# Splitting the spectrum tile z: the upper fifteen frequencies in a tile of their own, by channel

## Chip, core and metric

The kernel runs on one core of a Trainium2 chip. The metric is device time in microseconds of one execution. The engines are named as the profile names them: PE multiplies matrices (PEld is its load of the stationary operand), DVE, ACT and POOL work on elements, SP issues most of the transfers. ACT and POOL issue some too, and that time is not counted as busy.

## The reference

Four batches of 10048 positions and 128 channels go through a gated long convolution and then a hierarchical mixture of experts:

```
u = x * v
y = irfft(rfft(u, 2S) * rfft(h_filt, 2S))[:S]      # per channel, h_filt from a small network
x = x * y                                          # 40192 rows of 128
group = argmax(x @ w_group); expert = argmax(x @ w_expert[group])
out = g_w * e_w * (relu(x @ w1[expert]) @ w2[expert])
```

## The kernel before

A sequence is cut into 79 blocks of 128 positions, and the transform is done in two factors by matrix products in fp32. `dft_blocks` takes three channels a step (43 steps for 128 channels): 12 matmul instructions against `self.fa` turn 96 blocks into 79 complex numbers each, 158 columns per channel, in a tile `psa` of PSUM. One copy (L397) then writes them to `self.z`, a tile of [128 positions, 80 frequencies, 2 parts, 128 channels]; the 80th frequency is zero. `middle` takes two frequencies a step: `dft_positions` (L471) multiplies the 256 numbers of each frequency in z, as moving operand, by `bt`, then DVE and POOL multiply by the spectrum of the filter, and `back` (L641) multiplies by `bp` and copies the result back to z (L648, ACT).

The way back needs z with frequencies on the partitions. `turned` does this for 12 channels at a time. For the frequencies below KM = 64 it is one transpose of 128x128 for each channel (L671): 64 frequencies with two parts are 128 rows. The upper 16 frequencies of a channel are 32 rows, and four channels are put on top of each other by four matmuls against the identity, each into 32 partitions (L661). PE records two instructions for each of those fp32 matmuls and one for a transpose. The turned blocks lie in `pt` (three buffers, shared by others of the pool `psT`) and go by ACT (L673) to `tt`: first the upper frequencies of all 12 channels, 384 columns, then three blocks of 512. `inverse_blocks` (L696, L704) multiplies `tt` by `self.fi` into `po`, ACT makes `oo` of it (L713, L714), DVE `yt` and the product `xy` (L719, L721).

The stages follow each other. The network of the filter, its transform and its spectrum come first, then the transform of batch 0 and its middle. For each further batch one mixed stage does the transform of that batch (L392, L442, L453, L455 prepare it) together with the way back of the batch before, and a middle follows, with the routing of the batch before in it. After the last middle only the way back of batch 3 is left, and then the experts, page by page of 256 rows. For the text below: F is the filter's transform (43 to 78 us), D the transform of batch 0 (118 to 176), M0 to M3 the middles (176, 361, 586 and 822 on), X1 to X3 the mixed stages (250 to 361, 466 to 586, 695 to 822), T the last way back (924 to 999), E the experts (1029 on).

The order on an engine is made when the program is built, except where a line fixes it: the framework lets an instruction overtake others of its engine where data allow. Waits between engines follow from the tiles.

Of the kernel before, what the change touches and what calls it, by code (L numbers as in the profile page):

```python
# [12 lines left out]
F32 = mybir.dt.float32  # L13
# [12 lines left out]
SEQ, D, NB, N1 = 10048, 128, 79, 157  # L26
KM = 64
# [105 lines left out]
def groups(n, step):  # L133
    return [(i, min(step, n - i)) for i in range(0, n, step)]
# [5 lines left out]
class Kernel:  # L140
# [60 lines left out]
    def conv(self, ctx, right):  # L201
        tc, nc, d = self.tc, self.nc, self.d
        cp = ctx.enter_context(tc.tile_pool(name="cconst", bufs=1))
        zp = ctx.enter_context(tc.tile_pool(name="z", bufs=1))
# [3 lines left out]
        self.psr = lambda shape, name: self.psO.tile(shape, F32, tag="po", name=name)  # L208
        self.fa = cp.tile([NR, 2, 2 * NB], F32, name="fa")

        self.z = zp.tile([128, KM + 16, 2, 128], F32, name="z")
        nc.vector.memset(self.z[:, NB:], 0.0)
        ahead = ExitStack()
        made, folded = [], []
        with ExitStack() as c2:
# [12 lines left out]
        for b in range(self.nbat + 1):  # L228
# [41 lines left out]
            if not last:  # L270
                back = []
                for i, (k0, n) in enumerate(groups(NB, 2)):
                    back.append(self.middle(b, k0, n))
                    if len(back) > LAG:
                        self.back(*back.pop(0))
                    if b == 1 and i % 4 == 1:
                        self.clear_rest(i // 4)
                    self.scatter(i % 4 != 3)
                    if i % 4 != 3 if i < 30 else i % 2:
                        next(routing, None)  # L280
                for args in back:
                    self.back(*args)
# [101 lines left out]
    def dft_blocks(self, b, eo, d0, n, other=False):  # L384

        nc = self.nc
        pool, tag = (self.psA, "ps") if b not in ("h", 0) or d0 // GD % 2 else (self.psT, "pt")
        ps = pool.tile([128, GD, 2 * NB], F32, tag=tag, name="psa")
        for i in range(n):

            for h, hs in enumerate(HALVES):
                nc.tensor.matmul(  # L392
                    ps[hs, i], eo[:, i, hs], self.fa[:, h], start=True, stop=True
                )
        copy = nc.vector.tensor_copy if other else nc.scalar.copy

        ins = copy(  # L397
            self.z[:, :NB, :, d0 : d0 + n].rearrange("p k s d -> p (k s) d"),
            ps[:, :n].rearrange("p d c -> p c d"),
        )  # L400
        self.pace = ins
        self.in_turn(b, ins)
        self.tc.declare_no_dep(ins.ins, group=f"z{b}", reason="every step has channels of its own")
        self.tc.add_to_no_dep_group(f"z{b}", ins.ins)

    def run_ahead(self, b, i, made, folded):

# [57 lines left out]
    def dft_positions(self, k0, n, bt, other=False):  # L465

        nc = self.nc
        pool, tag = (self.psT, "pt") if other else (self.psA, "ps")
        ps = pool.tile([128, 2, 2, 128], F32, tag=tag, name="psb")
        for i in range(n):  # L470
            nc.tensor.matmul(  # L471
                ps[:, i],
                bt[:, i],
                self.z[:, k0 + i],
                start=True,
                stop=True,
            )
        return ps

    def parts(self, pool, src, tag, bufs=1, lo=None):  # L480

        nc, shape = self.nc, list(src.shape)
        parts = [pool.tile(shape, F32R, tag=f"{tag}{i}", name=f"{tag}{i}", bufs=bufs) for i in range(2)]
        nc.scalar.copy(parts[0], src)
        (lo or nc.gpsimd).tensor_tensor(parts[1], src, parts[0].bitcast(F32), ALU.subtract)
        return parts
# [149 lines left out]
    def back(self, k0, n, bp, y):  # L636

        nc = self.nc
        po = self.psT.tile([128, 2, 2, 128], F32, tag="pt", name="pbp")
        for i in range(n):  # L640
            nc.tensor.matmul(  # L641
                po[:, i].rearrange("p s d -> p (s d)"),
                bp[:, i],
                y[:, i].rearrange("p s d -> p (s d)"),
                start=True,
                stop=True,
            )
        self.pace = nc.scalar.copy(self.z[:, k0 : k0 + n], po[:, :n])  # L648

    def turned(self, d0, n):  # L650


        nc = self.nc
        tts = []
        for s, m in [(None, n // 4)] + groups(n, 4):
            pt = self.psT.tile([128, 4, 128], F32, tag="pt", name="pt")
            for i in range(m):
                if s is None:

                    for c in range(4):  # L660
                        nc.tensor.matmul(  # L661
                            pt[32 * c : 32 * c + 32, i],
                            self.z[:, KM:, :, d0 + 4 * i + c].rearrange("p k s -> p (k s)"),
                            self.ident,
                            start=True,
                            stop=True,
                            tile_position=(0, 32 * c),
                        )
                else:
                    src = self.z[:, :KM, :, d0 + s + i].rearrange("p k s -> p (k s)")  # L670
                    nc.tensor.transpose(pt[:, i], src, self.ident)  # L671
            tt = self.sp.tile([128, 4, 128], F32, tag="tt", name="tt", bufs=NTT)
            nc.scalar.copy(tt[:, :m], pt[:, :m])  # L673
            tts.append(tt)
        return tts
# [748 lines left out]
```

## Time and profile before

| | us |
|---|---|
| median of 3 runs | 2085.32 (2081.45 to 2090.16) |
| profiled execution | 2083.48 |
| its span | 2081.7 |

| engine | busy us | share |
|---|---|---|
| PE | 1962.0 | 94% |
| PEld | 1803.8 | 87% |
| DVE | 1626.1 | 78% |
| ACT | 1444.8 | 69% |
| POOL | 1333.4 | 64% |

Half of the span is stage E, where PE hardly pauses. The other half is the convolution, with four kinds of stages whose limits differ, so that the shares above say little: a stage is read by its own windows, and within it by who waits for whom. The busy time of PE in a window is the union of its instructions; the end of a matmul is modelled and contains the time until its last column is out.

### The profile page before, as it was taken

The numbers are of one execution on the slowest core, as the hardware profiler recorded it, in microseconds if no ns is written. First come the engines' busy times: TensorE is split into PE (matmuls) and PEld (weight loads), VectorE is DVE, ScalarE is ACT, GpSimd is POOL, SyncE is SP. The second block draws the span as 40 slices with busy tenths as digits, with TensorE's granted clock in tenths as the row PEclk, the third lists the DMA queues.
The fourth block names the chain that finished last, engine by engine and source line by source line (L and its number), as shares of the span: only waits on it lengthen the run. The fifth ranks groups of instructions, "written<-read, shape, count | busy, mean of one in ns | idle before, by whom it ended". The sixth has DMA issues, their size and how long they took to land.

```text
span 2081.7 us, 54011 instructions
## 1 busy us (share of the span) xinstructions
PE 1962.0 (94%) x18062; PEld 1803.8 (87%) x18062; DVE 1626.1 (78%) x3432; ACT 1444.8 (69%) x3210; POOL 1333.4 (64%) x1371
## 2 busy tenths in 40 slices
PE   8988999979999789989899999999999999999997
PEld 7867888767787578768699999999999999999997
DVE  5587765687658765796599998889999998888885
ACT  6652477436753466436688788888888888888886
POOL 3157600665689657976357677888888886555554
PEclk9999999999999799999899999999999999999999
DMA  4699965976889578968544455555555554443442
GB/s 136 226 263 267 275 168 160 333 226 174 229 301 296 157 190 254 339 198 277 188 126 136 134 154 151 155 180 169 157 161 155 161 150 131 125 134 121 127 126 66
DMA packets 258721, 388.93 MB, mean 187 GB/s; under 512 B 32680, under 2 KB 132627, under 8 KB 258433
## 3 DMA queue, kind: packets, MB, share of 16 engines
q1 hardware_dynamic: 225024, 318.01, 50.8%
q0 software_dynamic: 23904, 51.83, 7.0%
q10 hardware_dynamic: 9504, 15.54, 2.8%
q8 instruction: 146, 2.39, 0.5%
q14 instruction: 143, 1.16, 0.2%
HBM read 303.24 MB, written 83.04 MB: 186 GB/s over the span
## 4 chain that ended last, share of the span: by engine, by line
PE 50%; DVE 2%; POOL 2%; issue 1%; DMA 1%; ACT 0%; SPq 0%; DVEq 0%; ACTq 0%; POOLq 0%
PE py L1293 7%; PE py L1291 7%; PE py L1292 7%; PE ph L1272 7%; PE ph L1274 7%; PE ph L1273 7%; PE ptm L1305 2%; PE px L1229 2%; POOL wl L1261 1%; POOL out L1317 1%; PE pt L671 1%; PE ptr L786 1%; PE po L696 0%; PE po L704 0%; DMA mw<-m_w 0%
## 5 line engine op out<-in xcount | busy, mean ns | idle before, releaser
L1281 DVE SCALAR_TENSOR_TENSOR hl<-ph,hh 128x512 fp32r<-128x512 f32 x656 | 445.2, 683 | 93.3 <-ACT hh L1280 92.5
L1280 ACT ACTIVATE hh<-ph 128x512 fp32r<-128x512 f32 x656 | 395.6, 603 | 138.8 <-PE ph L1274 71.9
L358 POOL DMA_INDIRECT prow<-stg,adr x316 | 355.1, 1124 | 136.4 <-issue 63.6
L1317 POOL DMA_INDIRECT out<-os,to x328 | 349.0, 1064 | 91.6 <-issue 72.5
L1291 PE MATMUL py<-hh,wh 128*128 128x256 f32 x1312 | 398.7, 304 | 0.0
L1272 PE MATMUL ph<-xh,wh 128*128 128x256 f32 x1312 | 373.5, 285 | 5.4 <-ACT wh L1254 2.8
L1293 PE MATMUL py<-hh,wl 128*128 128x256 f32 x1312 | 373.2, 284 | 5.5 <-POOL wl L1261 5.5
L1274 PE MATMUL ph<-xh,wl 128*128 128x256 f32 x1312 | 373.4, 285 | 0.4 <-DVE wl L1261 0.4
L1273 PE MATMUL ph<-xl,wh 128*128 128x256 f32 x1312 | 372.9, 284 | 0.0
L1292 PE MATMUL py<-hl,wh 128*128 128x256 f32 x1312 | 371.4, 283 | 0.0
L1261 POOL TENSOR_TENSOR wl<-ws,wh 128x512 fp32r<-128x512 f32 x162 | 220.1, 1359 | 202.1 <-ACT wh L1254 200.9
L1293 PEld LDWEIGHTS py<-hh,wl 128*128 128x128 f32 x1312 | 251.4, 192 | 8.4 <-POOL wl L1261 8.4
L1272 PEld LDWEIGHTS ph<-xh,wh 128*128 128x128 f32 x1312 | 252.8, 193 | 6.1 <-ACT wh L1254 3.0
L1274 PEld LDWEIGHTS ph<-xh,wl 128*128 128x128 f32 x1312 | 253.1, 193 | 0.9 <-DVE wl L1261 0.8
L1273 PEld LDWEIGHTS ph<-xl,wh 128*128 128x128 f32 x1312 | 253.2, 193 | 0.1
L1292 PEld LDWEIGHTS py<-hl,wh 128*128 128x128 f32 x1312 | 252.8, 193 | 0.0
L1291 PEld LDWEIGHTS py<-hh,wh 128*128 128x128 f32 x1312 | 252.0, 192 | 0.0
L1261 DVE TENSOR_TENSOR wl<-mw,wh 128x512 fp32r<-128x512 f32 x328 | 238.1, 726 | 0.0
L648 ACT COPY z<-pbp 128x512 f32<-128x512 f32 (+1 forms) x160 | 92.6, 579 | 207.1 <-PE pbp L641 204.2
L630 POOL TENSOR_TENSOR y<-t 128x256 f32<-128x256 f32 (+1 forms) x160 | 121.2, 757 | 159.5 <-DVE t L629 153.9
L471 PE MATMUL psb<-z,bt 128*128 128x256 f32 x790 | 201.1, 387 | 8.6 <-DMA bt<-c_b 2.8
L1254 ACT CAST wh<-mw 128x512 fp32r x328 | 206.6, 630 | 0.0
(232 smaller groups left out, 4339.7 us busy)
## 6 DMA issues: line engine op xcount, KB each, us to landing
ws<-m_w SPq DMA_DIRECT2D x328, 256.0 KB
ht<-hspec SPq DMA_DIRECT2D x156, 256.0 KB
xv<-xv_in SPq DMA_DIRECT2D x131, 288.0 KB
bt<-c_b SPq DMA_DIRECT2D x95, 256.0 KB
xg<-prow SPq DMA_DIRECT2D x164, 130.0 KB
bp<-c_bp SPq DMA_DIRECT2D x76, 256.0 KB
stg<-xyd SPq DMA_DIRECT2D x76, 256.0 KB
xyd<-xy SPq DMA_DIRECT2D x57, 256.0 KB
```

The source lines that it names most:

```text
L358: ins = self.nc.gpsimd.indirect_dma_start(self.d["prow"], bass.IndirectOffsetOnAxis(ap=u.adr[:, t : t + 1], axis=0), u.rows[:, t - u.t0], ...
L1254: k.fix(k.nc.scalar.copy(hi, self.matrix(i, half, self.ea)))
L1261: ins = v.tensor_tensor(lo, self.matrix(i, half, self.ed), self.wh[i][half].bitcast(F32), ALU.subtract)
L1272: k.fix(nc.tensor.matmul(ph[:, j], wh, self.xh, start=True, stop=False))
L1273: k.fix(nc.tensor.matmul(ph[:, j], wh, self.xl, start=False, stop=False))
L1274: k.fix(nc.tensor.matmul(ph[:, j], wl, self.xh, start=False, stop=True))
L1280: k.fix(nc.scalar.activation(hh, ph, AF.Relu))
L1281: k.fix(nc.vector.scalar_tensor_tensor(hl, ph, 0.0, hh.bitcast(F32), ALU.max, ALU.subtract))
L1291: k.fix(nc.tensor.matmul(self.py, wh, self.hh[c], start=(c == 0), stop=False))
L1292: k.fix(nc.tensor.matmul(self.py, wh, self.hl[c], start=False, stop=False))
L1293: k.fix(nc.tensor.matmul(self.py, wl, self.hh[c], start=False, stop=(c == NC - 1)))
L1317: ins = k.nc.gpsimd.indirect_dma_start(k.d["out"], bass.IndirectOffsetOnAxis(ap=self.to[:, h : h + 1], axis=0), o[:, h], None, bounds_chec ...
```

## The change

The tile z keeps the 64 lower frequencies, in the layout that it had. The upper 15, and a sixteenth that is zero, move to a new tile `zr` of [128 positions, 128 channels, 16 frequencies, 2 parts]. For four channels its 128 numbers then lie next to each other, and one transpose turns them. Both tiles together have the size of z before.

- `dft_blocks` copies `psa` in two instructions on the same engine: 384 elements per partition to z, and three runs of 30 to zr.
- `dft_positions` reads a frequency above 63 from zr: 128 pairs, 128 bytes apart. Its result stands in `psb` as before, so that the output of the matmul now goes by channel: neighbouring columns lie 512 bytes apart.
- `back` lays `pbp` out by channel for these frequencies: the matmul's output has a step of 16 bytes, and ACT's copy writes runs of four numbers to zr.
- `turned` issues one transpose for four channels in place of four matmuls.

```
-        self.z = zp.tile([128, KM + 16, 2, 128], F32, name="z")
-        nc.vector.memset(self.z[:, NB:], 0.0)
+        self.z = zp.tile([128, KM, 2, D], F32, name="z")
+        self.zr = zp.tile([128, D, 16, 2], F32, name="zr")
+        nc.vector.memset(self.zr[:, :, NB - KM :], 0.0)
...
-        ins = copy(
-            self.z[:, :NB, :, d0 : d0 + n].rearrange("p k s d -> p (k s) d"),
-            ps[:, :n].rearrange("p d c -> p c d"),
-        )
+        main = self.z[:, :, :, d0 : d0 + n].rearrange("p k s d -> p (k s) d")
+        rest = self.zr[:, d0 : d0 + n].rearrange("p d k s -> p d (k s)")[:, :, : 2 * (NB - KM)]
+        for name, to, at in (
+            ("z", main, ps[:, :n, : 2 * KM].rearrange("p d c -> p c d")),
+            ("zr", rest, ps[:, :n, 2 * KM :]),
+        ):
+            ins = copy(to, at)
...
         for i in range(n):
             nc.tensor.matmul(
-                ps[:, i],
+                self.by_channel(k0, ps)[:, i],
                 bt[:, i],
-                self.z[:, k0 + i],
+                self.frequency(k0 + i),
...
+    def frequency(self, k):
+        return self.z[:, k] if k < KM else self.zr[:, :, k - KM]
+    def by_channel(self, k, t):
+        return t if k < KM else t.rearrange("p i s d -> p i d s")
...
+        po = self.psT.tile([128, 512], F32, tag="pt", name="pbp")
+        if k0 < KM:
+            po = po.rearrange("p (i s d) -> p i s d", i=2, s=2)
+        else:
+            po = po.rearrange("p (d i s) -> p i s d", i=2, s=2)
...
+            to = self.zr[:, :, k0 - KM : k0 - KM + n]
+            self.pace = nc.scalar.copy(to, po[:, :n].rearrange("p i s d -> p d i s"))
...
-                    for c in range(4):
-                        nc.tensor.matmul(
-                            pt[32 * c : 32 * c + 32, i],
-                            self.z[:, KM:, :, d0 + 4 * i + c].rearrange("p k s -> p (k s)"),
-                            self.ident,
-                            start=True,
-                            stop=True,
-                            tile_position=(0, 32 * c),
-                        )
+                    src = self.zr[:, d0 + 4 * i : d0 + 4 * i + 4].rearrange("p d k s -> p (d k s)")
+                    nc.tensor.transpose(pt[:, i], src, self.ident)
```

PE in a mixed stage, at one turn of 12 channels. `psa` is the transform of the next batch, `pt` the turned block, `po` the way back. Before:

```order
L392 MATMUL psa<-fa,eo 64x158 x6
L661 MATMUL pt<-ident,z 32x128 x12
L671 MATMUL pt<-ident,z 128x128 x12
L392 MATMUL psa<-fa,eo 64x158 x6
L696 MATMUL po<-fi,tt 64x316 x2
```

and with the change, at the same place:

```order
L393 MATMUL psa<-fa,eo 64x158 x6
L680 MATMUL pt<-ident,zr 128x128 x3
L683 MATMUL pt<-ident,z 128x128 x12
L393 MATMUL psa<-fa,eo 64x158 x6
L708 MATMUL po<-fi,tt 64x316 x2
```

Twelve matmuls became three transposes, and their neighbours stayed.

ACT in the same stage, from the second `oo` of a turn to the copies of the turned blocks (`tt`). `z` and `zr` are the copies of the transform, `xv` the sign change of the next input. Before:

```order
L714 COPY oo<-po 64x474
L397 COPY z<-psa 128x158x3
L453 ACTIVATE xv<-xv 96x3x64
L673 COPY tt<-pt 128x384
L453 ACTIVATE xv<-xv 96x3x64
L673 COPY tt<-pt 128x512 x3
```

and with the change, in X1 and X2:

```order
L726 COPY oo<-po 64x474
L404 COPY z<-psa 128x128x3
L404 COPY zr<-psa 128x3x30
L685 COPY tt<-pt 128x384
L685 COPY tt<-pt 128x512 x3
L457 ACTIVATE xv<-xv 96x3x64
```

The copy of the transform is two, and both sign changes that stood ahead of the last `tt` copies stand behind them or elsewhere in the turn.

PE at the end of a middle, where the last frequencies pass (`psb` forward, `pbp` back). Before:

```order
L471 MATMUL psb<-z,bt 128x256 x2
L641 MATMUL pbp<-y,bp 128x256 x2
L471 MATMUL psb<-z,bt 128x256 x2
L641 MATMUL pbp<-y,bp 128x256 x2
L471 MATMUL psb<-z,bt 128x256
```

and with the change:

```order
L475 MATMUL psb<-zr,bt 128x128x2 x2
L657 MATMUL pbp<-y,bp 128x2x128 x2
L475 MATMUL psb<-zr,bt 128x128x2 x2
L657 MATMUL pbp<-y,bp 128x2x128 x2
L475 MATMUL psb<-zr,bt 128x128x2
```

The order is the same; the operands are read, and the results written, with steps.

## Rows read from the trace of the kernel before

**Rows 1.** Busy time by stage: window, us, engines in us, granted clock, DMA share.

```profile
core 0: us, PE busy (x) PEld busy (x) DVE busy (x) ACT busy (x) POOL busy (x), PEclk, DMA share, GB/s
...
43.30:78.20 34.90, 34.57 (x512) 34.28 (x512) 14.35 (x22) 13.93 (x22) 0.00 (x0) 1.00 0.34 115
...
117.70:175.60 57.90, 47.98 (x513) 38.00 (x513) 46.62 (x78) 22.70 (x40) 41.57 (x61) 0.94 1.09 252
175.60:250.30 74.70, 70.19 (x318) 59.11 (x318) 54.23 (x87) 23.16 (x42) 57.25 (x82) 1.00 0.87 281
250.30:360.80 110.50, 104.85 (x1577) 92.75 (x1576) 68.40 (x122) 84.75 (x169) 1.42 (x3) 1.00 0.59 165
...
466.20:585.70 119.50, 109.60 (x1577) 96.31 (x1576) 76.52 (x157) 83.45 (x167) 73.61 (x73) 0.96 0.72 201
585.70:695.00 109.30, 94.29 (x585) 72.83 (x581) 87.99 (x187) 41.47 (x98) 96.99 (x117) 0.95 0.88 291
695.00:822.30 127.30, 115.30 (x1580) 99.79 (x1580) 83.44 (x181) 84.76 (x167) 78.80 (x75) 0.91 0.68 191
...
924.20:998.80 74.60, 71.46 (x1068) 60.59 (x1068) 47.43 (x103) 49.10 (x85) 44.24 (x43) 0.97 0.78 256
...
1029.00:2081.70 1052.70, 1028.12 (x8534) 1023.11 (x8534) 909.39 (x1908) 873.68 (x1971) 739.46 (x663) 0.99 0.47 142
```

**Rows 2.** Groups of the convolution, PE: busy us, mean ns, idle before.

```profile
L671 PE MATMUL pt<-ident,z 128*128 128x128 f32 x512 | 97.9, 334 | 26.7 <-ACT tt L673 26.4
...
L671 PEld LDWEIGHTS pt<-ident,z 128*128 128x128 f32 x512 | 82.8, 251 | 38.7 <-ACT tt L673 32.0 <-issue 2.1
...
L661 PE MATMUL pt<-ident,z 128*32 128x128 f32 x1024 | 45.5, 306 | 1.8 <-ACT z L648 1.8
...
L786 PE MATMUL ptr<-ident,xy 128*128 128x128 f32 x237 | 35.4, 273 | 0.0
...
L786 PEld LDWEIGHTS ptr<-ident,xy 128*128 128x128 f32 x237 | 29.2, 140 | 6.0 <-issue 0.6
```

**Rows 3.** The same view, copies out of PSUM on ACT.

```profile
L397 ACT COPY z<-psa 128x474 f32<-128x474 f32 x181 | 112.7, 642 | 63.6 <-PE psa L392 61.9
...
L673 ACT COPY tt<-pt 128x512 f32<-128x512 f32 x128 | 69.4, 596 | 3.0 <-PE pt L671 3.0
...
L803 ACT COPY lt<-plt 128x128 f32<-128x128 f32 x71 | 19.3, 272 | 0.7 <-PE plt L794 0.5
...
L673 ACT COPY tt<-pt 128x384 f32<-128x384 f32 x40 | 19.1, 476 | 3.2 <-PE pt L661 3.0
```

**Rows 4.** PE's waits in X1, X2, X3: us in total, times, longest.

```profile
PE pt L671 <- ACT tt L673: 4.6, 7, 1.5
...
PE pt L671 <- ACT tt L673: 9.8, 8, 3.7
...
PE pt L671 <- ACT tt L673: 12.0, 7, 3.8
```

**Rows 5.** Timeline of one turn in X1: start, us, work, idle before.

```profile
291.15 0.99 PE L661 MATMUL pt<-ident,z 128*32 128x128 f32 x24
...
292.08 1.44 PE L671 MATMUL pt<-ident,z 128*128 128x128 f32 x8
...
292.59 0.56 DVE L442 TENSOR_TENSOR xv<-xv 96x384 f32<-96x384 f32 x1 [1.56 <-DMA xv<-xv_in]
...
293.38 0.46 ACT L673 COPY tt<-pt 128x384 f32<-128x384 f32 x1
...
293.89 0.86 PE L671 MATMUL pt<-ident,z 128*128 128x128 f32 x4 [0.37 <-ACT tt L673]
```

**Rows 6.** The chain that ended last, within T: shares of T by line.

```profile
by line: PE pt L671 15.0%; PE po L696 13.9%; PE po L704 11.9%; DMA mw<-m_w 10.2%; PE pt L661 8.2%; issue 8.1%; DVE yt L719 6.6%; DVE lt L943 2.4%; DVE f L925 2.4%; DVE lt L934 2.2%; DVE f L937 2.0%; DVE other L951 1.9%; DVE f L947 1.8%; POO
```

**Rows 7.** Timeline in M3: two unbroken runs of fp32 matmuls.

```profile
913.51 1.03 PE L641 MATMUL pbp<-y,bp 128*128 128x256 f32 x4
...
914.80 1.89 PE L641 MATMUL pbp<-y,bp 128*128 128x256 f32 x8
```

More of the change, by code (lines that the diff above doesn't have):

```diff
@@ L395, in dft_blocks @@
         copy = nc.vector.tensor_copy if other else nc.scalar.copy
-        ins = copy(
-            self.z[:, :NB, :, d0 : d0 + n].rearrange("p k s d -> p (k s) d"),
-            ps[:, :n].rearrange("p d c -> p c d"),
-        )
+        main = self.z[:, :, :, d0 : d0 + n].rearrange("p k s d -> p (k s) d")
[5 more added lines that the diff above has]
+            ins = copy(to, at)
+            self.in_turn(b, ins)
+            self.tc.declare_no_dep(ins.ins, group=f"{name}{b}", reason="every step has channels of its own")
+            self.tc.add_to_no_dep_group(f"{name}{b}", ins.ins)
         self.pace = ins
-        self.in_turn(b, ins)
-        self.tc.declare_no_dep(ins.ins, group=f"z{b}", reason="every step has channels of its own")
-        self.tc.add_to_no_dep_group(f"z{b}", ins.ins)
     def run_ahead(self, b, i, made, folded):
@@ L638, in back @@
         nc = self.nc
-        po = self.psT.tile([128, 2, 2, 128], F32, tag="pt", name="pbp")
+        po = self.psT.tile([128, 512], F32, tag="pt", name="pbp")
[3 more added lines that the diff above has]
+            po = po.rearrange("p (d i s) -> p i s d", i=2, s=2)
         for i in range(n):
             nc.tensor.matmul(
-                po[:, i].rearrange("p s d -> p (s d)"),
+                po[:, i],
                 bp[:, i],
-                y[:, i].rearrange("p s d -> p (s d)"),
+                y[:, i],
                 start=True,
@@ L647, in back @@
             )
-        self.pace = nc.scalar.copy(self.z[:, k0 : k0 + n], po[:, :n])
+        if k0 < KM:
+            self.pace = nc.scalar.copy(self.z[:, k0 : k0 + n], po[:, :n])
+        else:
+            to = self.zr[:, :, k0 - KM : k0 - KM + n]
+            self.pace = nc.scalar.copy(to, po[:, :n].rearrange("p i s d -> p d i s"))
     def turned(self, d0, n):
@@ L658, in turned @@
                 if s is None:
-                    for c in range(4):
-                        nc.tensor.matmul(
-                            pt[32 * c : 32 * c + 32, i],
-                            self.z[:, KM:, :, d0 + 4 * i + c].rearrange("p k s -> p (k s)"),
-                            self.ident,
-                            start=True,
-                            stop=True,
-                            tile_position=(0, 32 * c),
-                        )
+                    src = self.zr[:, d0 + 4 * i : d0 + 4 * i + 4].rearrange("p d k s -> p (d k s)")
+                    nc.tensor.transpose(pt[:, i], src, self.ident)
                 else:
-                    src = self.z[:, :KM, :, d0 + s + i].rearrange("p k s -> p (k s)")
+                    src = self.z[:, :, :, d0 + s + i].rearrange("p k s -> p (k s)")
                     nc.tensor.transpose(pt[:, i], src, self.ident)
```

## The prediction

> **What bounds the kernel now.** I read the busy time by stage first, because the change touches the convolution alone and stage E, half of the span, has nothing of it: PE is busy 1028.1 of its 1052.7 us [rows 1]. In the convolution PE looks like the limit of X1 to X3 too (104.9 of 110.5, 109.6 of 119.5, 115.3 of 127.3 us), and of T (71.5 of 74.6) [rows 1]. That share misleads, since an instruction is counted until its last column is out. So I read PE's waits next. In each mixed stage it stops at one place: the last four of twelve transposes wait for ACT's first `tt` copy, 7, 8 and 7 times in 11 turns, 4.6, 9.8 and 12.0 us in total [rows 4]. One turn of X1 shows why [rows 5]: PE issues the upper frequencies at 291.15 and eight transposes from 292.08, and then needs a fourth `pt` buffer; there are three, and ACT, which works in order, copies the first only at 293.38. ACT is busy 77% of X1 [rows 1] and is itself held by inputs: DVE's product of x and v stood still 1.56 us for a transfer in that turn [rows 5]. So the mixed stages run at the pace of a ring of transfer, DVE, ACT and PE, and PE has a little slack in it. In T there is no transform; its chain lies 49% on PE, 8.2% of 74.6 us (6.1 us) on the very matmuls that the change takes out [rows 6].
>
> **What PE saves.** 1024 recorded instructions of L661 take 45.5 us [rows 2], for 128 groups of four channels: 0.355 us a group. In their place stand 128 transposes. Their operand lies contiguous, as in L786: 35.4 us for 237, 0.149 us each; at the rate of L671, whose operand jumps 512 bytes from number to number, it would be 97.9 / 512 = 0.191 [rows 2]. I take the first: the loads say that the jump is what costs (251 ns against 140 for the same 128 columns [rows 2]). PE saves 128 x 0.206 = 26.4 us of work, 6.6 in each of X1, X2, X3 and T.
>
> Of that lands on the path:
> - T: the chain holds 6.1 us of L661; 0.149 / 0.355 of it stays, so 3.5 us go. A part of the turns is then caught by the POOL and the transfers in the same chain (the transfer of the experts' weights alone has 10.2% [rows 6]). I take 3.
> - X1 to X3: in 22 of 33 turns PE arrives earlier at a buffer that ACT has not freed, and waits longer; nothing is won there. In the other 11 turns at most 3 x 0.206 = 0.6 us each, 6.8 in all; I take half, 3.5.
>
> **What the second copy costs.** ACT's copies cost by element: 476 ns for 384, 596 for 512, 272 for 128 [rows 3], 0.82 ns an element on a base of about 165. The main copy has 384 elements, so 476; the rest 90, about 240, at most 272. The pair is 716 to 748 against 642 [rows 3]: 0.07 to 0.11 us more, and 0.18 if the 642 contains waiting. It happens 43 times in each of X1 to X3, so ACT gets 3 to 8 us more work in each, beside 25.8, 36.0 and 42.5 us in which it is idle [rows 1]. On the path it counts where PE waits for ACT: in the new order the pair stands directly ahead of the first `tt` copy, 22 turns x 0.13 = 3 us. The two sign changes that stood there move behind; that frees `pt` earlier and releases the next input later, and I set it at zero, as one wait against the other, with 3 us either way in each stage. In D, copies are hidden for the most part (ACT 22.7 of 57.9 us, DVE 46.6 [rows 1]); I take 0.5. In F ACT and DVE are busy 14 of 34.9 us [rows 1] and PE sets the end: 34 us of PE cover 21 to 22 copies on each, and nothing is lost unless PE were to wait for `psa`.
>
> **What the stepped operands cost.** Frequencies 64 to 78 now run through matmuls with a stepped moving operand and a stepped output: 15 x 5 forward (the filter and four batches) and 15 x 4 back, 135 fp32 matmuls, 270 recorded instructions. Contiguous, one takes (1.89 - 1.03) / 4 = 0.215 us [rows 7] for 256 columns, 0.84 ns a column. No row shows a stepped matmul. The near rows stand on two sides. ACT reads `psa` out of PSUM with a step of 632 bytes and writes runs of three, and takes 642 ns for 474 elements, where contiguous it takes 596 for 512 [rows 3]; by the element 1.35 against 1.16 ns, of which most is the base: a step costs there 0 to 0.1 us in 474. PE's loads of single numbers 512 bytes apart take 251 ns, contiguous ones 140 [rows 2], a factor of 1.8; in busy time of the transposes it is 0.191 against 0.149, a factor of 1.28. So the bounds are 270 x 0 and 270 x 0.215 x 0.79 = 46 us. A gain is excluded: nothing gets shorter. I take zero, because the new operand moves pairs and not single numbers, and because an fp32 column has 0.84 ns, the time that ACT has for an element when it takes steps for nothing. The copy back has 512 elements as before and runs of four: zero by the row with runs of three.
>
> The Trainium skill, "Advanced Engine Details and Errata", section PSUM Cachelines, says otherwise: "Any non-contiguous AP significantly slows down matmuls". By it the sum would end on the slow side, between the bounds of the second rival below; no row of this trace has a matmul to which it applies. For reads the skill ("SBUF — State Buffer", Specifications (TRN2)) asks for two hits in a 16-byte line for full bandwidth; the loads of single numbers in rows 2 agree that one is too few, and the pairs of zr would do.
>
> **Sum.** -3 (T) - 3.5 (X1 to X3, PE) + 3 (X1 to X3, ACT) + 0.5 (D) + 0 (stepped matmuls) = -3 us against the profiled execution of 2083.5: 2080.5. That execution lies 1.8 us under the median of its runs, so about 2082 against 2085.3. About 0.5% (10.4 us) is what a measurement can tell from no change.
>
> **Rivals.**
> - *PE is the limit after all* and its whole saving lands: for it, 92 to 96% busy in X1 to X3 and T [rows 1], and the sign changes that no longer stand ahead of the `tt` copies, which pays for a part of the pair. Against it, the 22 waits. 2085.3 - 26.4 + 3 = 2062. Chance 0.18.
> - *A stepped matmul is slower* (PSUM written, or SBUF read, in single places). Price: at the factor 1.8 of the loads 46 us, at 1.28 some 16 (270 x 0.215 x 0.28), nearly all on the path, since PE is busy 70.2 of 74.7 us in M0 and waits for nobody there for long, a little less in M2 (94.3 of 109.3, POOL 97.0) [rows 1]. Time 2082 + 16 to 46 = 2098 to 2128. It decides from (10.4 + 3) / 270 = 0.05 us an instruction, a quarter more than 0.215. Against it, what ACT shows for steps. Chance 0.25. The sentence of the Trainium skill quoted above speaks for it.
> - *ACT becomes the limit* of X1 to X3: its in-order list holds `tt`, `oo`, the sign changes and now 43 more copies; if all of 43 x 0.18 in each lands, 23 us, 2085.3 + 23 - 6.5 = 2102. Against it, its idle time. In X3 the new order has one turn in which two pairs of `oo` come between the `tt` copies, as there is one unruly turn before. Chance 0.07.
> - *The change doesn't do what it says:* excluded, the built order shows three transposes for twelve matmuls.
>
> **Chances and range.** The forecast has 0.50, its own range is 2072 to 2092. The lower rival reaches to 2062, half of it above 2066; the upper ones to 2128, with a third above 2115. The range 2066 to 2115 leaves out some 0.1 on either side. Faster by over 0.5% are most of the first rival and a corner of the forecast: 0.19. Slower by over 0.5% are the second and third: 0.31. Within: 0.50.
>
> **What would show it.** Right, if the transposes of zr take near 0.15 us each in busy time, T is about 3 us shorter, X1 to X3 are within 4 us of before with more waiting of PE for `tt`, and `psb` from zr takes as long as from z. Wrong, if the runs of `psb` or `pbp` in the last eighth of a middle are longer per instruction than 0.215 (second rival, M0 to M3 longer by 5 to 10 us each), if X1 to X3 shrink by 6 us each (first), or if they grow with ACT over 85% busy (third).

## The result, and the profile after the change

The changed kernel took 2047.43 us (median of 4 runs, 2042.33 to 2053.79) against 2083.39 for the kernel before (4 runs on the same chip, 2079.32 to 2090.16): a ratio of 0.983 with a 95% interval of 0.981 to 0.986. It is faster by 36 us where the forecast was no change, and it lies below the range. The profiled execution took 2044.59 us, its span 2042.7, against 2081.7 before.

The first view is again busy time by stage. The windows are F, D, M0, X1, X2, X3, T and E, as in [rows 1]; after a window and its length stand PE, PEld, DVE, ACT and POOL in us with their instructions, then the granted clock and the DMA share.

```profile
core 0: us, PE busy (x) PEld busy (x) DVE busy (x) ACT busy (x) POOL busy (x), PEclk, DMA share, GB/s
...
42.70:77.50 34.80, 34.52 (x512) 34.23 (x512) 15.02 (x42) 14.43 (x44) 0.00 (x0) 1.00 0.34 115
...
116.30:174.30 58.00, 47.57 (x513) 37.23 (x513) 45.51 (x87) 23.45 (x74) 41.88 (x61) 0.97 1.11 250
174.30:248.80 74.50, 70.20 (x318) 59.10 (x318) 54.20 (x87) 23.07 (x43) 57.15 (x82) 1.00 0.88 282
248.80:348.40 99.60, 97.59 (x1353) 86.97 (x1352) 65.26 (x122) 81.64 (x212) 1.45 (x3) 1.00 0.66 183
...
452.50:561.80 109.30, 101.63 (x1353) 90.25 (x1352) 70.75 (x157) 82.02 (x210) 68.50 (x73) 0.97 0.78 221
...
670.00:791.90 121.90, 110.57 (x1357) 96.09 (x1357) 78.63 (x181) 82.07 (x210) 72.55 (x75) 0.89 0.71 199
...
893.90:961.50 67.60, 65.01 (x844) 54.51 (x844) 43.10 (x102) 45.33 (x85) 42.63 (x43) 0.98 0.84 282
...
990.40:2042.70 1052.30, 1027.49 (x8534) 1022.47 (x8534) 907.60 (x1908) 872.76 (x1971) 738.94 (x663) 0.99 0.47 142
```

Against [rows 1] the gain stands in four stages: X1 110.5 to 99.6, X2 119.5 to 109.3, X3 127.3 to 121.9, T 74.6 to 67.6. That is 33.5 of the 39.0 us of the span. F, D, M0 and E stayed within 0.4 us. In the four stages PE's busy time fell from 401.2 us (104.85 + 109.60 + 115.30 + 71.46) to 374.8, by 26.4 us, the figure that the prediction had worked out (how far by luck is said further down). The time fell by 7 us more than that: waits went along with the work.

The groups of the convolution, PE and ACT: busy us, mean ns of one, idle before. They answer [rows 2, 3].

```profile
L680 PE MATMUL pt<-ident,zr 128*128 128x128 f32 x128 | 24.6, 299 | 1.8 <-ACT zr L668 1.8
...
L680 PEld LDWEIGHTS pt<-ident,zr 128*128 128x128 f32 x128 | 13.6, 144 | 11.8 <-issue 7.1 <-ACT zr L668 3.8
...
L404 ACT COPY z<-psa 128x384 f32<-128x384 f32 x181 | 98.7, 546 | 67.3 <-PE psa L393 63.9
...
L404 ACT COPY zr<-psa 128x90 f32<-128x90 f32 x181 | 43.3, 239 | 0.0
...
L475 PE MATMUL psb<-z,bt 128*128 128x256 f32 x640 | 159.3, 381 | 5.9 <-DMA bt<-c_b 2.8 <-DVE hs L616 1.7 <-ACT zr L404 0.6
...
L475 PE MATMUL psb<-zr,bt 128*128 128x256 f32 x150 | 40.3, 389 | 1.2 <-DVE t L644 0.6 <-DVE hs L619 0.4 <-PE psb L475 0.2
```

The transposes of zr load at 144 ns, like the contiguous ones of L786 and not like the 251 of L671. In busy time, though, one of them takes 24.6 / 128 = 0.192 us and not the 0.149 of the prediction. The stepped matmul (`psb` from zr) takes 389 ns where the contiguous one takes 381; in the first experiment below the same two groups take 382 and 390, so the stepped operands cost nothing that matters. The two copies take 546 + 239 = 785 ns where one took 642 [rows 3], and the stages got shorter all the same.

Now the waits in X1, which the prediction read only for PE. Each row is an engine and line, what it waited for, us in total, times, longest. First the kernel before; its row for PE stands in [rows 4].

```profile
DVE eo L455 <- PE psa L392: 15.8, 19, 1.9
DVE xv L442 <- DMA xv<-xv_in: 14.2, 20, 1.8
...
ACT xv L453 <- DVE xv L442: 11.0, 9, 2.4
...
ACT oo L713 <- PE po L704: 4.1, 5, 1.1
```

In the same window, the queue that issues the input transfers:

```profile
SPq L437 <- DVE eo L455: 75.3, 36, 3.8
```

X1 after the change:

```profile
DVE xv L446 <- DMA xv<-xv_in: 20.9, 24, 1.5
ACT oo L725 <- PE po L716: 10.2, 16, 1.1
DVE eo L459 <- PE psa L393: 7.0, 14, 1.9
...
ACT xv L457 <- DVE xv L446: 1.0, 2, 0.8
...
PE pt L683 <- ACT tt L685: 0.8, 2, 0.5
```

PE's wait for ACT, which was to grow, fell from 4.6 to 0.8 us. ACT's wait for DVE ahead of its sign changes (`xv`) fell from 11.0 to 1.0, DVE's wait for PE's `psa` from 15.8 to 7.0; in their place ACT now waits more for PE's `po`. DVE's wait for the input transfers, from which the prediction let its ring start, rose from 14.2 to 20.9 us while the stage got 10.9 us shorter, so the transfers did not set the pace. They hang on the ring themselves: before the change their queue stood for DVE's `eo` 36 times, 75.3 us in all, because `eo` frees the buffer that the next input goes to.

This view counts only idle time after the modelled end of a matmul, and so it hides a part of PE's wait; the loads of the same transposes (PEld) wait for `tt` nine times in X1, 2.8 us in all. By the starts of the instructions, from the first of the twelve transposes of z to the next `psa`, the change takes 2.19 us in the turn below (296.44 to 298.63), and 1.86 us where there is no wait (307.96 to 309.82 in the run with four `pt` tiles, further down). Added up in this way over ten turns, PE's wait fell from 7.1 to 3.5 us: it was halved and did not go.

A turn of X1 shows it (timeline: start, us, work, idle before); it answers [rows 5].

```profile
295.61 0.56 ACT L725 ACTIVATE oo<-po 64x474 f32<-64x474 f32 x1 [0.73 <-PE po L716]
...
296.06 0.55 PE L680 MATMUL pt<-ident,zr 128*128 128x128 f32 x3
296.19 0.58 ACT L726 COPY oo<-po 64x474 f32<-64x474 f32 x1
...
296.44 2.26 PE L683 MATMUL pt<-ident,z 128*128 128x128 f32 x12
296.80 0.48 ACT L404 COPY z<-psa 128x384 f32<-128x384 f32 x1
...
297.17 0.25 ACT L404 COPY zr<-psa 128x90 f32<-128x90 f32 x1
297.30 2.03 ACT L685 COPY tt<-pt 128x384 f32<-128x384 f32 x4
...
298.63 1.03 PE L393 MATMUL psa<-fa,eo 96*64 96x158 f32 x12
...
305.27 0.55 PE L680 MATMUL pt<-ident,zr 128*128 128x128 f32 x3
```

ACT's way to the first `tt` copy (`oo`, `oo`, `z`, `zr`) begins at 295.61 with a wait that PE's `po` ends. So in this turn ACT is late because PE is: the next turn starts 9.21 us on, where a turn took some 10.2 before.

### The profile page after: what moved, and what is told of

It is laid out like the page before. It is cut to its first block, busy times and chain, and to the rows that moved or that the text cites. A ratio compares the mean times of both kernels' runs of the same rounds, so it can differ in the third digit from the quotient of the medians.

```text
span 2042.7 us, 52533 instructions
## 1 busy us (share of the span) xinstructions
PE 1931.5 (95%) x17166; PEld 1778.1 (87%) x17166; DVE 1604.6 (79%) x3462; ACT 1434.3 (70%) x3395; POOL 1320.1 (65%) x1371
## 4 chain that ended last, share of the span: by engine, by line
PE 50%; POOL 2%; DVE 1%; ACT 1%; DMA 1%; issue 1%; ACTq 0%; DVEq 0%; SPq 0%; POOLq 0%
PE py L1305 8%; PE py L1303 7%; PE py L1304 7%; PE ph L1286 7%; PE ph L1284 7%; PE ph L1285 7%; PE ptm L1317 2%; PE px L1241 2%; POOL wl L1273 1%; POOL out L1329 1%; PE po L708 1%; PE po L716 1%; PE ptr L798 0%; PE pt L683 0%; DMA mw<-m_w 0%
## 5 line engine op out<-in xcount | busy, mean ns | idle before, releaser
L359 POOL DMA_INDIRECT prow<-stg,adr x316 | 347.1, 1098 | 126.5 <-issue 50.1
L1329 POOL DMA_INDIRECT out<-os,to x328 | 347.9, 1061 | 91.5 <-issue 71.9
L1266 ACT CAST wh<-ws 128x512 fp32r<-128x512 f32 x328 | 204.8, 624 | 1.3 <-DMA ws<-m_w 1.3
L393 PE MATMUL psa<-fa,eo 96*64 96x158 f32 x2048 | 182.6, 312 | 13.9 <-POOL eo L464 4.7
```

What stands on the lines that cost most here:

```text
L359: ins = self.nc.gpsimd.indirect_dma_start(self.d["prow"], bass.IndirectOffsetOnAxis(ap=u.adr[:, t : t + 1], axis=0), u.rows[:, t - u.t0], ...
L1266: k.fix(k.nc.scalar.copy(hi, self.matrix(i, half, self.ea)))
L1329: ins = k.nc.gpsimd.indirect_dma_start(k.d["out"], bass.IndirectOffsetOnAxis(ap=self.to[:, h : h + 1], axis=0), o[:, h], None, bounds_chec ...
```

## The experiments

They ran on other chips than the first comparison, on which the kernel before took 2133 to 2135 us (medians of 13 to 23 runs). X1, with almost no work on POOL, takes the same there: the change had 99.8 us against 99.6. It is therefore the stage in which kernels are compared. The ratios are to the kernel before on the same chip; they carry the spread of E, which none of these kernels touches and which took 1061 to 1080 us there.

Two limits hold for all that follows. Each kernel is built anew, and the order on its engines is made again. The traces show where it moved in X1: the kernel before, the layout with four matmuls and the kernel before with ACT's new order have one order on PE, and the change has the same with three transposes in place of twelve matmuls. But the change with ACT's old order and the one with a third copy on ACT have another order on PE, and the one with its transposes issued three times has another order on ACT. Each is said in its place. And X2 and X3 aren't separated by these runs: on these chips X2 took 121 to 122 us with the change and 123 to 126 with four matmuls, X3 131 to 134 and 130 to 132. Their gains, and that of T, rest on the one pair of profiles above.

| kernel | X1, us | ratio to before, 95% interval |
|---|---|---|
| before (first chip) | 110.5 | 1 |
| the change (first chip) | 99.6 | 0.983 (0.981 to 0.986) |
| the change, second and third time | 99.8, 99.8 | 0.986 (0.981 to 0.990), 0.988 (0.984 to 0.992) |
| its layout, with four matmuls | 109.4 | 0.995 (0.993 to 0.997) |
| before, with ACT's new order | 110.5 | 0.999 (0.997 to 1.001) |
| the change, with ACT's old order | 101.5 | 0.993 (0.990 to 0.995) |
| all frequencies by channel | 102.4 | one run |
| transposes three times | 108.0 | 0.994 (0.990 to 0.997) |
| a third copy on ACT | 102.1 | 0.986 (0.982 to 0.991) |
| the change, four `pt` tiles | 96.0, 97.5 | 0.985 (0.980 to 0.990), 0.986 (0.982 to 0.990) |
| before, four `pt` tiles | 106.0 | 0.997 (0.993 to 1.000) |

**The layout and both copies, but the four matmuls.** Does the new home of the upper frequencies help by itself?

```diff
-                    nc.tensor.transpose(pt[:, i], src, self.ident)
+                    for c in range(4):
+                        nc.tensor.matmul(pt[32 * c : 32 * c + 32, i],
+                            self.zr[:, d0 + 4 * i + c].rearrange("p k s -> p (k s)"),
+                            self.ident, start=True, stop=True, tile_position=(0, 32 * c))
```

> The change with everything but its transposes: the two tiles, the two copies per step and the stepped matmuls stay, but the upper frequencies are turned by four matmuls per four channels, as before. The built order of ACT is that of the kernel before (15 sign changes of a batch stand ahead of the third turn's first tt copy, 16 ahead of the second). If the layout costs nothing (as the profile of the change suggests for the stepped matmuls, 389 ns a piece from zr against 381 from z), this runs like the kernel before, 2083 us, X1 110 to 112 us. If the second copy costs what I charged (3 us in X1 to X3) it is 2086. If the gain of the change comes from the layout itself (faster copies, or loads of the 32-column operands that now lie contiguous), it is 2060 or less.

X1 came to 109.4 us, nearly all of the way back to 110.5, and the ratio to 0.995. So tile, copies and stepped operands are worth little in X1, and the replaced matmuls are worth most. The layout is not worth nothing. With a contiguous operand the four matmuls take PE 0.79 us to the next group for twelve channels, where they took 0.95 before and the transposes take 0.38: 0.16 of the 0.57 us comes from the layout. And by the whole time this kernel is 6 to 15 us faster than the one before (0.993 to 0.997); X1 shows 1.1 us of that, and where the rest lies its one profile can't tell.

**ACT's order alone.** The built order of the change sets two sign changes behind the `tt` copies that they stood ahead of. Here the kernel before gets that order.

```diff
-            nc.scalar.activation(both[:, :, 128:192], hi, AF.Copy, scale=-1.0)
+            ins = nc.scalar.activation(both[:, :, 128:192], hi, AF.Copy, scale=-1.0)
+            turn = (d0 // GD - 6) // 4
+            if turn >= 0:
+                self.after(ins, self.copies[turn, 3])
```

> The kernel before, its old tile and its four matmuls, but with ACT's order of the change in X1 to X3: a sign change that stands behind a turn's tt copies in the change is held behind them here too. Theory PE (PE is the limit of the mixed stages, its saved work lands whole, the order is a by-product): no change, 2083 us, X1 110 us. Theory order (the sign changes held up the first tt copy, so PE stood for a pt buffer 4.6, 9.8 and 12.0 us): most of that waiting goes, X1 106 us, X2 112, X3 121, together some 10 to 15 us less, 2070 us. T stays at 74.6 us in both.

X1 stayed at 110.5 us. PE's wait for `tt` fell from 4.6 to 3.0 us, so the order reaches its target; ACT still waits for DVE as long as before.

```profile
DVE eo L459 <- PE psa L393: 14.5, 16, 2.2
...
ACT xv L454 <- DVE xv L443: 11.5, 9, 2.0
...
PE pt L675 <- ACT tt L677: 3.0, 7, 1.3
```

That the stage is no shorter at all is due to one turn of 12.8 us, where the others take 9.2 to 10.2. In it the granted clock was 0.66 over 5 us, a mix of its two levels (2.4 and 1.2 GHz), and PE had been busy for only 3.89 of the 5 us before; in X1 of the kernel before it was 1.00 throughout [rows 1].

```profile
333.10:338.10 5.00, 4.78 (x44) 4.01 (x46) 2.50 (x5) 3.39 (x9) 0.00 (x0) 0.66 0.50 146
```

With a turn like the others X1 would be about 108 us (an estimate: 110.5 less 12.8, plus 10.1). So the order alone is worth 0 to 3 us here, less than the 4.5 that its theory asked for.

**The change without ACT's new order.** The first two `tt` copies of a turn are held behind the sign changes, as before.

```diff
+            ins = nc.scalar.activation(both[:, :, 128:192], hi, AF.Copy, scale=-1.0)
+            turn, at = divmod(d0 // GD - 6, 4)
+            if turn >= 2 and at < 2:
+                self.after(self.copies[turn, at], ins)
```

> The change with ACT's old order in X1 to X3: the sign changes that stood ahead of the first and of the second tt copy stand there again. Theory PE: as fast as the change, 2047 us, X1 100 us. Theory order: PE's waiting for tt comes back and takes what the transposes saved, X1 105 us or more, X2 115, X3 125, 2060 us. The ring of my prediction (nothing of PE's saving lands in the 22 waiting turns) asks for more: X1 108, 2070 us. T stays at 67.6 us in all.

X1 took 101.5 us, 1.9 us more than the change. That is not ACT's order alone, because PE was built in another order too: two instructions of the next `psa` stand between the eighth and the ninth transpose of z, and further on `psa` and `po` alternate. In this order PE stood for `tt` only 0.6 us in X1, and seven of ten turns took 9.48 us, where those of the change take 9.2. With the two runs above that is all four corners of matmuls and order (110.5 and 109.4 with four matmuls, 101.5 and 99.6 with transposes), in this one with PE's order changed along: the matmuls decide. By the whole time it is 6.5 us faster than the layout with four matmuls on the same chip (2115.9 and 2122.4 us), where X1 alone is 7.9 us shorter; X3 was 140.1 us in its one profile, and that was not followed up.

**PE's time given back.** Each transpose of zr is issued three times into the same place.

```diff
+                    for again in range(3):
+                        nc.tensor.transpose(pt[:, i], src, self.ident)
```

> Each transpose of the upper frequencies is issued three times in a row into the same place, so that TensorE has 6 more of them in a turn and everything else stays as in the change, the copies and their sizes too. The three of a turn take 0.38 us to the start of the next group, so this adds 0.76 us to TensorE's work in each of the 11 turns of a mixed stage and of T, more than the 0.57 us that the change took away. Theory (TensorE's work lands whole): X1 +8 us (107 to 109), T +6 to +8, X2 and X3 +6 to +8 each, +28 in all. Rival (TensorE has a wait for the first tt copy in most turns, which takes up what is added or removed): X1 +0 to +3, +0 to +10 in all.

X1 rose by 8.2 us to 108.0, where the theory had 107 to 109. The window, and then the waits of the same stage:

```profile
247.60:355.60 108.00, 104.26 (x1417) 93.86 (x1416) 65.54 (x122) 83.08 (x212) 1.39 (x3) 1.00 0.61 169
```

```profile
DVE eo L459 <- PE psa L393: 17.5, 17, 1.9
...
ACT xv L457 <- DVE xv L446: 12.0, 11, 2.8
...
PE pt L684 <- ACT tt L686: 2.5, 2, 1.9
```

A typical turn took 9.8 us where the change's takes 9.2: 0.65 us more, as much as PE's group of three grew (1.04 us to the next group instead of 0.38). The rest of the 8.2 us is one turn of 11.7 us with a wait of 1.9. The waits of the kernel before are back with it (DVE for PE 15.8 then, 17.5 here; ACT for DVE 11.0 and 12.0). But ACT was built in another order than in the change: both sign changes stand ahead of the first `tt` copy in nine of eleven turns, where the change has one of them ahead of it in the first turn and none later. So it isn't shown that PE's length alone makes these waits, nor that it alone makes the turn longer. Elsewhere the theory was too high: beside the change on the same chip X2 rose by 2.1 us (121.9 to 124.0), X3 by 2.9 and T by 2.4, not by 6 to 8 each. The whole time rose by 29 us (medians of 2095.5 and 2124.5), near the 28 of the theory, but in the two profiles half of that lies in E (1061 and 1077 us), which neither touches.

**ACT's time taken away.** A third copy in each step, into a scratch tile.

```diff
+            if name == "zr" and b in (1, 2, 3) and not other:
+                again = self.sp.tile([128, GD, 30], F32, tag="again", name="again", bufs=1)
+                copy(again[:, :n], at)
             ins = copy(to, at)
```

> In X1 to X3 ScalarE makes its small copy of the upper frequencies twice in each step, once into a scratch tile: 4 more copies of 0.24 us in a turn, 0.96 us a turn, 10.3 us in each mixed stage, 31 in all. TensorE's instructions are the change's, and ScalarE's order otherwise too. ScalarE is busy for 81.6 of X1's 99.6 us in the change, so it has 18 us to spare. Theory (TensorE is the limit, ScalarE's chain ahead of tt waits for TensorE rather than the other way round): X1 +0 to +3, +0 to +10 in all. Rival (the turn is as long as ScalarE's chain to the first tt copy): X1 +8 to +10, +25 to +31 in all.

```profile
250.40:352.50 102.10, 100.78 (x1354) 90.67 (x1353) 64.77 (x122) 87.73 (x255) 1.42 (x3) 1.00 0.64 179
```

43 more copies (212 to 255 on ACT) lengthened X1 by 2.3 us, not by 10, though they are 0.96 us more of ACT in each of 10.7 turns. Even the 2.3 us are not ACT's time: PE's order is the one of the run with ACT's old order, with `psa` between the eighth and the ninth transpose,

```profile
300.55 0.48 PE L393 MATMUL psa<-fa,eo 96*64 96x158 f32 x2
300.96 0.85 PE L686 MATMUL pt<-ident,z 128*128 128x128 f32 x4
```

and most turns take the same 9.48 us as there, without a third copy. PE stands for `tt` 0.3 us in the whole stage. Against that run (101.5 us) the third copy cost 0.6 us in X1, and X2 and X3 did not grow. So in this order on PE the turn is not as long as ACT's work; with the change's own order on PE this was not tried.

**The wait for `tt` taken away.** With four `pt` tiles PE needs no copy inside a turn's twelve transposes. One bank moves from `psa` to `pt`, in the change and in the kernel before.

```diff
-        self.psA = ctx.enter_context(tc.tile_pool(name="psA", bufs=3, space=PSUM, reuse_waits="tile"))
-        self.psT = ctx.enter_context(tc.tile_pool(name="psT", bufs=3, space=PSUM, reuse_waits="tile"))
+        self.psA = ctx.enter_context(tc.tile_pool(name="psA", bufs=2, space=PSUM, reuse_waits="tile"))
+        self.psT = ctx.enter_context(tc.tile_pool(name="psT", bufs=4, space=PSUM, reuse_waits="tile"))
```

> The change with one PSUM bank moved from the pool of the psa tiles (3 to 2) to that of the pt tiles (3 to 4), so that a turn's fourth transposed group doesn't wait for the turn's first tt copy. In the change TensorE waits for tt for 0.8 us in X1 and 7.5 us each in X2 and X3. Theory: those 7.5 us are the most that can come back in X2 and X3 and nothing in X1; with only two psa tiles TensorE's next psa waits for ScalarE's copies of the one before last, which took 0.55 + 0.24 us and can cost up to 0.4 us in each of 43 steps a stage. So X1 +0 to +6, X2 and X3 -7 to +6, and in all -10 to +20. Rival (the tt copy sets the turn): X1 to X3 shorter by 4 to 10 each, -12 to -30 in all.

> The kernel before with one PSUM bank moved from the psa tiles (3 to 2) to the pt tiles (3 to 4), as in the run of the change with four pt tiles, whose X1 took 96.0 us with turns of 8.87 us and no wait of TensorE in them. TensorE's part that the change replaced is 0.95 us a turn here and 0.38 there, everything else in a turn was alike. Theory (the gain is the sum of TensorE's shorter work and of a wait for tt that shrank): without the wait a turn here is 8.87 + 0.57 = 9.44 us and X1 102 to 103, so that the replaced matmuls alone are worth 6.3 us of X1's 10.9 and the wait the rest. Rival (the change won by its order of ScalarE's work or by its copies): X1 within 2 us of 96 or still 108 and over.

The timeline of PE in a turn of the change with four `pt` tiles (start, us, work), which runs from 307.58 to 316.45 without a gap:

```profile
307.58 0.55 PE L680 MATMUL pt<-ident,zr 128*128 128x128 f32 x3
307.96 1.92 PE L683 MATMUL pt<-ident,z 128*128 128x128 f32 x12
309.82 1.03 PE L393 MATMUL psa<-fa,eo 96*64 96x158 f32 x12
...
316.45 0.55 PE L680 MATMUL pt<-ident,zr 128*128 128x128 f32 x3
```

The same place in the kernel before with four `pt` tiles:

```profile
301.46 1.03 PE L661 MATMUL pt<-ident,z 128*32 128x128 f32 x24
302.42 2.02 PE L671 MATMUL pt<-ident,z 128*128 128x128 f32 x12
304.38 1.03 PE L392 MATMUL psa<-fa,eo 96*64 96x158 f32 x12
...
310.42 1.03 PE L392 MATMUL psa<-fa,eo 96*64 96x158 f32 x12 [0.15 <-ACT z L397]
311.38 1.01 PE L661 MATMUL pt<-ident,z 128*32 128x128 f32 x24
```

From the first transpose to the next `psa` it is 2.92 us with the matmuls of L661 and 2.24 with the transposes of zr: 0.68 us a turn, 7 us in X1's 10.7 turns. That is what PE's work is worth by itself, close to the 0.62 (3 x 0.206) of the prediction. But the two kernels differ by 10.0 us in X1 without the wait (106.0 and 96.0), about as much as with it (10.9). In the kernel before, PE now waits at another place, for ACT's copy of `psa` at 310.42; six of ten turns take 9.9 to 10.2 us and the others 9.4 to 9.6, where those of the change take 8.9. My number for the kernel before, 102 to 103, was too low for that reason. In both runs the measured X1 lies between theory and rival. The wait for `tt` is worth 4.5 us in the kernel before (110.5 to 106.0) and 2 to 4 in the change (the second of its runs has one turn of 10.8 us among those of 8.9). That is more than the 0.8 us which the view of the waits listed for the change and near the 3.5 by the starts. In the kernel before, the ring closes somewhere else when it goes.

> The change with four pt tiles and two psa tiles again, in more rounds beside the change itself, to see whether what it wins in the mixed stages reaches the end. X1 96 us, X2 and X3 together 5 to 12 us shorter than in the change beside it, T and R alike. Theory: 4 to 15 us shorter than the change in all. Rival (the length of the stage of the experts, which neither touches, varies by more than that from one execution to the next): within 5 us of the change.

> The change as it is, beside the run with four pt tiles. X1 99.5 to 100, its ratio to the kernel before 0.980 to 0.990.

In 6 runs of each, the change with four `pt` tiles took 2101.67 us and the change itself 2107.32; the first time it was 2098.55 and 2095.45. What it wins in X1 (2 to 4 us) and X2 (4 to 7) can't be told from no gain in the whole, so there is no version here that is shown to beat the change.

> The changed kernel as it is, beside the three that follow, so that their stages can be set against its own on one chip. On the chip of its first run X1 took 99.6 us, M0 74.6, M1 104.2, X2 109.2, X3 122.4 and T 67.6. Theory (TensorE is the limit of the mixed stages) and rival (ScalarE's first tt copy sets the turn) both expect X1 within 1.5 us of 99.6 again, since no stage from D to X1 has moved by more than 2 us between chips so far. The ratio to the kernel before should lie in 0.978 to 0.988.

The change repeated what it had shown: 0.986, with X1 at 99.8.

**All frequencies by channel.** z, too, lies by channel, so that every transpose has a contiguous operand and every matmul of the middles is stepped. (Here xy comes to lie over z in another order than before, and the last batch's output is not the reference's.)

```diff
-        self.z = zp.tile([128, KM, 2, D], F32, name="z")
+        self.z = zp.tile([128, D, KM, 2], F32, name="z")
```

> The change carried on: the lower 64 frequencies lie by channel too, so that all transposes load a contiguous operand, and all matmuls of the middles are stepped (pairs read 512 bytes apart, output columns 512 and 16 bytes apart). It leaves something out: in the last way back the product overwrites z before its channels are turned, so the rows of batch 3 are not the reference's, and T, the routing and E are not to be compared. X1 to X3 and M1 to M3 are. If PE is the limit of the mixed stages and a contiguous operand makes a transpose 0.149 us in place of 0.184, X1 loses 128 x 0.035 = 4.5 us, 95 us. If a stepped matmul costs anything, the middles show it: 316 instructions of each at 0.215 us, 7 us more in M1 for each tenth. If ACT is the limit by now, X1 stays at 99 us.

Its groups, where the first is the stepped matmul and the second the load of the contiguous transposes:

```profile
L475 PE MATMUL psb<-z,bt 128*128 128x256 f32 x640 | 161.7, 383 | 7.9 <-DMA bt<-c_b 2.7 <-ACT z L404 2.3 <-DVE hs L616 1.2
...
L677 PEld LDWEIGHTS pt<-ident,z 128*128 128x128 f32 x512 | 62.1, 151 | 56.2 <-ACT tt L679 41.7 <-POOL z L727 9.7 <-ACT zr L404 4.1
```

640 stepped matmuls take 383 ns against 381, so the second rival is ruled out on a far larger sample. The contiguous loads of L677 take 151 ns instead of 252 and PE's busy time in X1 falls from 97.6 to 94.2 us, but X1 is 102.4, not shorter: PE now waits for `tt` for 7.2 us, nine times. One turn took 12.2 us, with 1.9 of these and a granted clock of 0.66 over 5 us, after 5 us in which PE was busy for 3.06. The others have a median of 9.1 us against 9.2 in the change, so without it X1 would be about as long as the change's (an estimate: 102.4 less 12.2, plus 9.1).

```profile
DVE xv L446 <- DMA xv<-xv_in: 26.7, 26, 3.1
...
PE pt L677 <- ACT tt L679: 7.2, 9, 1.9
```

So the lock that the prediction saw does exist, one step further on: when PE gets shorter still, most of the saving is lost in a wait. Which of the ring's other members sets it there (the row above it hints at the input transfers, for which DVE waits longer than in any other of these runs, though 23.1 us of that wait in the change with four `pt` tiles cost PE nothing) was not tried.

## Why the prediction was wrong, step by step

**What bounds X1 to X3: the step that failed.** From [rows 4, 5] I read PE's wait for the first `tt` copy as slack in PE, so that earlier work in 22 of 33 turns would only wait longer. I followed that wait in one turn from PE to ACT, from ACT to DVE and from DVE to a transfer, took the pace to come from there, and stopped one link too early: I did not ask what DVE and the transfers wait for. DVE stood behind PE's `psa` (15.8 us), the largest wait of the stage, which was not in my rows at all, and the transfers behind DVE's `eo`. So the ring runs through PE. The saved work was not taken back by a longer wait: a turn of X1 fell from some 10.2 to 9.2 us, 0.68 us of it PE's own work, and the wait before the ninth transpose was halved (7.1 to 3.5 us in ten turns). Why it was halved stays open. ACT's new order, which I set at zero, has a part in it (0 to 3 us by itself), and the rest no run separates, since the kernels that were to do so got other orders on PE or ACT. The busy share of 92 to 96%, which I called misleading, was the better witness. Measured: 10.9, 10.2 and 5.4 us in X1 to X3 in place of 3.5 for all three.

**Two sizes.** PE's saving came out as I had it (26.4 us of work, found as 26.4; 0.62 us a turn, found as 0.68), in part by luck. By its group it is 45.5 - 24.6 = 20.9 us, since a transpose of zr has 0.192 us of busy time, the rate of L671 that I had turned down, and not 0.149; the transposes of z lost 3.7 us (97.9 to 94.2), in which waiting is counted too. On top of it came 3 to 4 us of waits in X1, which no rival of mine allowed for: the first one, "PE is the limit", took 3 us off for the copies and ended at 2062. The measured time lies 15 us below even that. 5.5 us of the span's gain lie outside X1 to X3 and T, 1 to 1.3 us each in M1, M2 and R; M1 was as short (104.1 and 104.2) in the first two kernels with four matmuls above, so I don't count this as the change's.

**T.** I took 3 of the 6.1 us that L661 had in the chain; T became 7.0 us shorter. The chain within T, by line, answers [rows 6]:

```profile
by line: PE po L708 18.2%; PE po L716 16.9%; PE pt L683 11.4%; DMA mw<-m_w 11.1%; issue 9.7%; DMA prow<-empty,fidx 7.9%; ACT oo L725 5.2%; ACT oo L726 4.8%; ACT tt L685 4.2%; DVE yt L731 2.7%; PE pt L680 2.3%; POOL z L733 1.9%; POOL prow L3
```

L680 has 2.3% of 67.6 us where L661 had 8.2% of 74.6 (1.6 and 6.1 us, 4.5 less), and the transposes of z fell from 11.2 to 7.7 us in it. The rest I can't assign: on the other chips T took 78.6 and 81.3 us with the change, 80.0 and 83.7 with four matmuls, so one profile of T is good to 2 or 3 us at best.

**ACT's second copy.** The pair costs 143 ns more than the single copy, near the 130 that I put on the path. The main copy takes 546 and not 476 ns. It reads with a step and writes with a jump of 512 bytes; with z by channel, where it does neither, it takes 478 in the run with all frequencies by channel.

```profile
L404 ACT COPY z<-psa 128x384 f32<-128x384 f32 x181 | 86.6, 478 | 73.0 <-PE psa L393 65.9 <-remote 3.1 <-PE po L710 1.3
```

But 3 us for X1 to X3 were too much: 0.96 us a turn of a third copy, 1.7 times what the change added (4 x 0.143), cost 0.6 us in X1 against the kernel with the same order on PE, and nothing that could be seen in X2 and X3. The third rival, ACT as the limit, finds no support in this.

**The stepped operands.** Right at nought, for the matmul forward (389 and 383 against 381 ns) and back (`pbp` 390 ns where all 632 are stepped, in the run with all frequencies by channel; 392 before); none of M0 to M3 is longer than before by more than 0.1 us. The Trainium skill's sentence that any non-contiguous access slows matmuls down ("Advanced Engine Details and Errata", PSUM Cachelines) does not hold for these fp32 matmuls, whose output and moving operand go in steps. The loads show what does depend on the step: 252 ns for a stationary operand with a jump of 512 bytes, 144 to 151 for a contiguous one.

**D and F.** As expected: 58.0 and 57.9 us, 34.8 and 34.9.

## What to carry to other kernels

A wait of the busiest engine is slack only if what it waits for is not itself waiting for that engine: follow the releaser's own waits, in order of size, and those of a transfer's queue too, until the chain either leaves the ring (the program's start) or comes back. If it comes back, the wait is no proof that shorter work is lost, and what it is worth has to be tried. To try it on the chip, issue the disputed instruction several times into the same place, copy something once more on the suspected engine, or take the wait away by one more buffer. Then compare the order on every engine with the kernel that it is set against, before the times are compared: here three kernels that were to differ in one thing were built with another order on PE or ACT. And read single turns beside the stage: four stages here were 2 to 3 us longer by one turn.

## What the runs showed of the hardware

An fp32 matmul of 256 columns runs at the same speed with pairs of numbers 128 or 512 bytes apart as its moving operand and with a stepped output: in the runs that have both, 382 to 404 ns in busy time (150 of them at a time; 383 for 640) against 381 to 390. As a stationary operand, single numbers 512 bytes apart took 252 ns to load, contiguous ones 144 to 151. Four matmuls of 32 columns each, into 32 partitions each, take longer than one transpose of the four together: 0.95 us to the next group for twelve channels, or 0.79 with a contiguous operand, against 0.38. And chips differ by stage: the same kernel took over 2% longer on three others, nearly all of it in X2, X3, T, E and the routing between these two (X2 121.9 us against 109.3, E 1061 to 1077 against 1052), while F, M0 and X1 agree within 1 to 3 us. In all the longer stages POOL writes with indirect transfers; but M3 has 31 of them too and agrees (101.7 us against 101.9), so why was not found.
